# Late pair slots of one and a half blocks, by turns with triples, and quarter-row gathers for slots 3 to 5

## The chip, the core and the metric

The kernel runs on one core of a Trainium2 chip. The metric is the device time of one execution in microseconds, of which the median over several runs is given. The engines are TensorE (PE, matrix products; PEld are its weight loads), VectorE (DVE), ScalarE (ACT), GpSimd (POOL) and SyncE (SP, which here only issues transfers). Transfers from SP and from POOL share the core's 16 DMA engines. On-chip memory has 128 partitions; products land in PSUM, in banks of 512 numbers per partition.

## The reference

An attention with 32 memory slots per head is computed for 8 batches of 576 positions and 8 heads of 64. Its output is the input x (4608 tokens of 512 numbers) of a mixture of 8 experts with a hidden size of 1024, where each token goes to the one expert of the largest gate logit:

```python
x = attn_out.transpose(0, 2, 1, 3).reshape(B * S, H * D)   # 4608 x 512
e_idx = argmax(x @ w_gate)                                  # one expert per token
for e in range(E):
    mask = e_idx == e
    h = maximum(x[mask] @ w1[e], 0)                         # 512 -> 1024
    out[mask] = gate_w[mask] * eom[mask, e] * (h @ w2[e])   # 1024 -> 512
```

All numbers are 32-bit. The kernel gets that precision from products of two parts: each matrix is split into a rounded part (`hh`, `xh`, `whl[:, 0]`) and the remainder (`hl`, `xl`, `whl[:, 1]`), and a product is made of three passes, high by high, low by high, high by low (`PASS`, L1151).

## The kernel before

**Attention.** The batches are handled in four pairs. Products, softmax and gate logits are issued in an order written out by hand (`ORDER`, `MEM`). The rows of x, each 512 numbers with four 16-number strips of gate values (`XROW`, 576 numbers), are stored to a buffer `xs` in DRAM. When a pair of batches is done, `rank` (L875) finds each token's expert and its rank within the expert, and builds one-hot masks `Aw` on POOL (L956).

**Slots.** The experts' work is cut into slots that are fixed in number while the program is written; which expert a slot serves is looked up when it runs (`slot`, read by `value_load`, L550). A block is 128 tokens of one expert. There are five early slots of three blocks (0 and 1 use list "a", 2 to 4 list "b", made once two and three of the four batch pairs are ranked), five late triples (slots 5 to 9), four pairs of two blocks (10 to 13), and 22 single-block slots at the end, which run only if `used` (L1315) says that blocks are left over. The late slots use list "l". `route_early` (L281) and `route_late` (L338) share the experts' blocks out; `table` (L213) makes the lists of token numbers: `idx_g` to gather by, `idx_o` to scatter by, and for list "l" `idx_q`, the indices by quarters of rows (L259 to L274), made with the matrix `rep`.

**Gather and turn.** `gather` (L512) brings a slot's rows from `xs` into `xg` by indirect DMAs on POOL's queue: one per block for the slots in `WHOLE` (0 to 5), or, for the others (`quart`), four per block, each of 32 tokens' four row quarters on 128 partitions. `turn_x` (L1021) turns x so that its 512 numbers lie on partitions, in four parts c: by PE transposes (L1041) for whole rows, by a DVE transpose of 32 x 32 squares (L1035) for quarters, where four small ACT copies also fetch the gate values (L1031). ACT rounds the result to `xh` (L1043), DVE takes the remainder `xl` (L1044). Three `xg` tiles go round; `gathers` (L587) issues a slot's gathers when its list is made (`listed`) and it is fewer than three slots ahead, and forces what is missing when it must.

**Weights.** A slot's weights come in 8 units of 512 KB: four of the first layer, four of the second. `Stream` (L534) loads them on SP's queue; `split` (L557) makes the two parts, a cast on ACT (L564) and a subtraction on DVE (L565). `done` (L579), called after each unit used, splits further units as far as the ring of split units allows (10 tiles after `GROW`).

**A slot's products.** `several` (L1160) runs triples and pairs. First layer: for each of the four units and each half j of it, 12 matmuls (L1176) of 384 or 256 columns into one bank; ACT evicts them through a relu (L1181) and DVE takes the remainder (L1182). Second layer: for each unit and block, six matmuls of 512 columns (L1198). `finish_y` (L1153) scales a finished block by its gate on ACT and scatters it to `out` (POOL, L1156). `TURN` says after which steps of the second layer the four parts of the next slot's x are turned (`nxt`).

**Order around the change.** Each engine runs its instructions in the order in which the program issued them. What is not part of the slots goes between their matmuls: `hook` (L1284), eight times in a first layer and once per step of a second, advances a clock by one tick and takes two steps of the routing generators (`late`). `hold(n)` lets such a generator wait n ticks, and `take_pr` lets it wait for the one shared PSUM tile `pr`. After slot 1 (`LAST`) `settle` (L1258) closes the attention's memory, opens pools for the rest, builds `rep` and grows the ring. At that time `rank(3)` with `route_late` is still under way.

Of the kernel before, what the change touches and what calls it, by code (L numbers as in the profile page):

```python
# [66 lines left out]
def attention_moe(tc, phiT, kv, qT, wgo, wall, out):  # L67
# [3 lines left out]
    with contextlib.ExitStack() as ctx:  # L71
# [21 lines left out]
        idx = {}  # L93
        for nm, n in (("a", 3 * NPS[0]), ("b", 3 * NPS[1]), ("l", NBL)):
            idx[nm] = (cp.tile([P, n], I32, name="idx_g" + nm), cp.tile([P, n], I32, name="idx_o" + nm),
                       cp.tile([P, 4, n], I32, name="idx_q" + nm) if nm == "l" else None)
# [116 lines left out]
        def table(nm, q, nch, nblk):  # L213
# [24 lines left out]
            hl = rt.tile([P, 2, NBL], BF16, name="hl_i")  # L238
# [11 lines left out]
            V.tensor_scalar(i2v, ivv, 0.0, 100000.0, ALU.is_equal, ALU.mult)  # L250
            yield
            V.scalar_tensor_tensor(io[:], ivv, -1.0, i2v, ALU.add, ALU.add)
            if nm != "l":
                return
            for z in order:
                if z["nm"] == nm and not z["quart"]:
                    z["listed"] = True

            rep = env["rep"]  # L259
            pq = ps_r.tile([P, 4, 2, NBL], F32, name="pr")  # L260
            for b in range(4):
# [19 lines left out]
        def route_early(k):  # L281
# [48 lines left out]
            yield  # L330
            yield from table(nm, t1, nch, 3 * n)
            for z in order[s0:s0 + n]:
                z["listed"] = True
            if k == 0:
                gathers(0)
            yield
# [1 line left out]
        def route_late():  # L338
# [159 lines left out]
        for s in range(NSLOT):  # L498
# [4 lines left out]
            else:  # L503
# [3 lines left out]
            slots.append({"s": s, "nb": nb, "q0": q0, "idx": idx[nm], "rows": rows,  # L507
                          "nm": nm, "quart": s not in WHOLE,
                          "known": False, "listed": False})
        order = slots  # L510

        def gather(z):  # L512
            z["xg"] = xgs.tile()
            for k in range(z["nb"]):
                q = z["q0"] + k
                if z["quart"]:
                    rows = 4 * z["rows"]
                    for b in range(4):
                        G.indirect_dma_start(  # L519
                            out=z["xg"][:, k, XQ * b:XQ * b + XQ], out_offset=None,  # L520
                            in_=xs[0:z["rows"]].rearrange("t (a q) -> (t a) q", a=4),
                            in_offset=bass.IndirectOffsetOnAxis(ap=z["idx"][2][:, b, q:q + 1], axis=0),
                            bounds_check=rows - 1, oob_is_err=False)
                    continue
                G.indirect_dma_start(
                    out=z["xg"][:, k], out_offset=None, in_=xs[0:z["rows"]],
                    in_offset=bass.IndirectOffsetOnAxis(ap=z["idx"][0][:, q:q + 1], axis=0),
                    bounds_check=z["rows"] - 1, oob_is_err=False)
# [492 lines left out]
        def turn_x(z, c):  # L1021


            nb, xg = z["nb"], z["xg"]
            n = nb * P
            if c == 0:
                z["x"] = (mo.tile([P, 4, 3 * P], F32R, name="xh"), mo.tile([P, 4, 3 * P], F32R, name="xl"))
                if z["quart"]:
                    z["g"] = env["xt"].tile([P, 3], F32, name="gx")
                    for b in range(4):  # L1030
                        A.copy(z["g"][32 * b:32 * b + 32, 0:nb], xg[0:32, 0:nb, XQ * b + P])  # L1031
            xh, xl = z["x"]
            if z["quart"]:
                xt = env["xt"].tile([P, 3 * P], F32, name="xt")
                V.transpose(xt[:, 0:n].rearrange("p (k i) -> p k i", i=32),  # L1035
                            xg[:, 0:nb].rearrange("p k (b q) -> p (k b) q", b=4)[:, :, 32 * c:32 * c + 32])
# [6 lines left out]
            A.copy(xh[:, c, 0:n], pt)  # L1043
            V.tensor_tensor(xl[:, c, 0:n], pt, xh[:, c, 0:n].bitcast(F32), ALU.subtract)  # L1044

        NT = 5 * NBP
        deferred = []
# [104 lines left out]

        def finish_y(z, k, py):  # L1153
            y = mo.tile([P, DM], F32, name="y", bufs=2)
            A.activation(y[:], py, AF.Copy, scale=z["g"][:, k:k + 1] if z["quart"] else z["xg"][:, k, P:P + 1])  # L1155
            G.indirect_dma_start(  # L1156
                out=out, out_offset=bass.IndirectOffsetOnAxis(ap=z["idx"][1][:, z["q0"] + k:z["q0"] + k + 1], axis=0),
                in_=y[:], in_offset=None, bounds_check=NTOK - 1, oob_is_err=False)

        def several(i, st, nxt, hook):  # L1160

            z = order[i]
            nb, x, h = z["nb"], z["x"], []
            n_ = nb * P
            for u in range(4):
                w = st.take(i, u)
                h_ = mo.tile([P, 2, 3 * P], F32R, name="hh", bufs=4)
                l_ = mo.tile([P, 2, 3 * P], F32R, name="hl", bufs=4)
                for j in range(2):
                    if nb == 3 or j == 0:  # L1170
                        pb = bank([1, 512] if nb == 3 else [2, 256], "ps")
                    n = 0
                    for cc in range(4):
                        for a, b in PASS:
                            o = cc * 256 + j * P
                            T.matmul(pb[:, j % pb.shape[1], 0:n_], w[:, b, o:o + P], x[a][:, cc, 0:n_],  # L1176
                                     start=(n == 0), stop=(n == 11))
                            n += 1
                    if nb == 3 or j == 1:
                        js = slice(j, j + 1) if nb == 3 else slice(0, 2)  # L1180
                        A.activation(h_[:, js, 0:n_], pb[:, :, 0:n_], AF.Relu)  # L1181
                        V.scalar_tensor_tensor(l_[:, js, 0:n_], pb[:, :, 0:n_], 0.0, h_[:, js, 0:n_].bitcast(F32),  # L1182
                                               ALU.max, ALU.subtract)
                    if j == 0:
                        hook()
                h.append((h_, l_))
                st.done(PUMP[0])
                hook()
            py = [bank([DM], "ps") for _ in range(nb)]

            turns = [(u, k) for u in range(4, 8) for k in range(nb)]
            if 8 * i + 8 == st.hi:
                turns.sort(key=lambda t: t[1])
            for step, (u, k) in enumerate(turns):
                w = st.take(i, u)
                for f in range(2):
                    for n, (a, b) in enumerate(PASS):
                        T.matmul(py[k], h[u - 4][a][:, f, k * P:(k + 1) * P], w[:, b, DM * f:DM * f + DM],  # L1198
                                 start=(u == 4 and f == 0 and n == 0), stop=(u == 7 and f == 1 and n == 2))
# [5 lines left out]
                if k == nb - 1:  # L1205
                    st.done(PUMP[0])

        def single(i, st, nxt):
# [49 lines left out]
        def settle():  # L1258
# [107 lines left out]
```

## Time and profile before

| | |
|---|---|
| runs of the kernel | 578.89 us median of 3 (578.73 to 579.51) |
| the profiled execution | 577.36 us, of which its instructions span 575.6 us |
| matmuls | 4031 |
| memory traffic in the span | 102.99 MB read, 20.87 MB written |
| indirect gathers by quarters, by whole rows | 80, 18 |
| mean granted clock of PE | 0.966 |

A row of a timeline gives start and length in microseconds, engine, line, operation, output <- input, shapes and count, and in brackets how long the engine had been idle before and what ended that. A row of a group gives the total busy time and the mean length of one in nanoseconds, then the idle time of the engine before them. A row of a stretch gives its length and the busy time of each engine in it, the granted clock, the busy share of the DMA engines and what they moved in GB/s. Matmuls overlap, so a matmul's listed length is longer than the distance to the next one.

### The profile page before, as it was taken

What the parts mean: (1) busy time and instruction counts of PE and PEld (TensorE: products, weight loads), DVE (VectorE), ACT (ScalarE), POOL (GpSimd) and SP (SyncE); (2) the same over time, 40 slices, a digit from 0 to 9 for tenths busy, and PEclk for the clock granted to TensorE, in tenths of its full rate; (3) what the DMA queues carried; (4) which work ended last, traced back from release to release, by engine and by line L of the source; (5) the groups of instructions that cost most, each with busy time, mean ns of one, the idle gap of its engine ahead of it and who ended that gap; (6) DMA issues with size and microseconds to landing.
All of it is one profiled execution on the core that took longest, in us unless ns stands there. A gap on an engine that the chain in (4) does not pass through costs nothing. (4 is left out here: it accounts for less than half of the span.)

```text
span 575.6 us, 10886 instructions
## 1 busy us (share of the span) xinstructions
PE 529.1 (92%) x4031; PEld 455.6 (79%) x4031; DVE 356.1 (62%) x736; ACT 280.4 (49%) x496; POOL 229.2 (40%) x253
## 2 busy tenths in 40 slices
PE   3688886789899999999999999999999999999993
PEld 2455554478689799898998989898998989899893
DVE  4485979767765659996443555646465555676610
ACT  3475655454254456453434545445454445656510
POOL 2242575831166034312471735547170604553011
PEclk9987879989899999999999999999999999999998
DMA  8999999975367659756564665656465655687000
GB/s 308 413 401 391 382 376 356 308 301 168 116 197 245 209 173 308 246 155 183 161 200 145 204 177 180 184 171 176 139 202 168 179 172 181 198 264 223 7 28 32
DMA packets 42238, 124.14 MB, mean 216 GB/s; under 512 B 10368, under 2 KB 10432, under 8 KB 41792
## 3 DMA queue, kind: packets, MB, share of 16 engines
q1 hardware_dynamic: 35136, 102.71, 54.7%
q0 software_dynamic: 7040, 20.65, 10.4%
q8 instruction: 33, 0.54, 0.4%
q14 instruction: 29, 0.24, 0.1%
HBM read 102.99 MB, written 20.87 MB: 215 GB/s over the span
## 5 line engine op out<-in xcount | busy, mean ns | idle before, releaser
L1176 PE MATMUL bps<-xh,whl 128*128 128x384 f32 (+1 forms) x896 | 213.6, 322 | 0.1
L1198 PE MATMUL bps<-whl,hh 128*128 128x512 f32 x608 | 197.7, 396 | 0.0
L565 DVE TENSOR_TENSOR whl<-w,whl 128x1024 fp32r<-128x1024 f32 x112 | 136.8, 1228 | 68.5 <-ACT whl L564 68.5
L1176 PEld LDWEIGHTS bps<-xh,whl 128*128 128x128 f32 x896 | 156.9, 190 | 1.9 <-issue 0.6
L1176 PE MATMUL bps<-xl,whl 128*128 128x384 f32 (+1 forms) x448 | 143.8, 321 | 0.0
L1198 PEld LDWEIGHTS bps<-whl,hh 128*128 128x128 f32 x608 | 114.7, 189 | 26.1 <-issue 2.5
L1198 PE MATMUL bps<-whl,hl 128*128 128x512 f32 x304 | 119.0, 391 | 0.0
L564 ACT CAST whl<-w 128x1024 fp32r<-128x1024 f32 x112 | 116.4, 1046 | 0.0
L519 POOL DMA_INDIRECT xg<-xs,idx_ql x80 | 90.2, 1127 | 25.2 <-issue 24.3
L1181 ACT ACTIVATE hh<-bps 128x384 fp32r<-128x384 f32 (+1 forms) x96 | 48.9, 510 | 96.9 <-PE bps L1176 96.7
L1182 DVE SCALAR_TENSOR_TENSOR hl<-bps,hh 128x384 fp32r<-128x384 f32 (+1 forms) x96 | 55.1, 577 | 52.1 <-ACT hh L1181 52.1
L1176 PEld LDWEIGHTS bps<-xl,whl 128*128 128x128 f32 x448 | 85.1, 190 | 0.5
L1156 POOL DMA_INDIRECT out<-y,idx_ol x23 | 24.9, 1081 | 127.1 <-ACT y L1155 101.4
L1198 PEld LDWEIGHTS bps<-whl,hl 128*128 128x128 f32 x304 | 57.5, 189 | 10.8
L838 POOL TENSOR_TENSOR ea<-ea,mx 128x512 f32<-128x512 f32 (+1 forms) x20 | 19.2, 961 | 49.8 <-DVE mx L836 45.4
L1043 ACT CAST xh<-xt 128x384 fp32r<-128x384 f32 (+1 forms) x32 | 14.7, 460 | 37.9 <-DVE xt L1035 37.9
L873 ACT COPY xo<-bpd 128x576 f32<-128x576 f32 x36 | 22.6, 640 | 21.3 <-PE bpd L871 12.7
L956 POOL TENSOR_SCALAR Aw<-iota_row,row 128x128 bf16<-128x128 bf16 x36 | 26.8, 759 | 12.4 <-DVE row L946 12.4
L871 PE MATMUL bpd<-ve_b,aT 64*128 64x144 f32 (+1 forms) x320 | 28.5, 327 | 2.4 <-DVE ea L833 2.4
L1044 DVE TENSOR_TENSOR xl<-xt,xh 128x384 fp32r<-128x384 f32 (+1 forms) x32 | 15.8, 492 | 24.1 <-ACT xh L1043 24.1
L1155 ACT ACTIVATE y<-bps,gx 128x512 f32<-128x512 f32 x20 | 13.4, 687 | 30.4 <-PE bps L1198 13.9
L871 PEld LDWEIGHTS bpd<-ve_b,aT 64*128 64x128 f32 (+1 forms) x320 | 21.7, 196 | 8.1 <-issue 3.5
(248 smaller groups left out, 471.6 us busy)
## 6 DMA issues: line engine op xcount, KB each, us to landing
w<-wall SPq DMA_DIRECT2D x112, 512.0 KB, 3.9
kvt<-kv SPq DMA_DIRECT2D x32, 512.0 KB, 7.5
xs<-xo SPq DMA_DIRECT2D x16, 576.0 KB, 5.8
qt<-qT SPq DMA_DIRECT2D x16, 512.0 KB, 9.1
ph<-phiT SPq DMA_DIRECT2D x3, 1152.0 KB, 12.1
kv<-kv SPq DMA_DIRECT2D x4, 512.0 KB, 9.0
xg<-xs,idx_ql POOLq DMA_INDIRECT x80, 4.2
ph<-phiT SPq DMA_DIRECT2D x4, 288.0 KB, 3.2
```

The lines of the kernel that those rows point to most:

```text
L519: G.indirect_dma_start(out=z["xg"][:, k, XQ * b:XQ * b + XQ], out_offset=None, in_=xs[0:z["rows"]].rearrange("t (a q) -> (t a) q", a=4), i ...
L564: A.copy(hl[:, 0], w[:])
L565: V.tensor_tensor(hl[:, 1], w[:], hl[:, 0].bitcast(F32), ALU.subtract)
L838: G.tensor_tensor(eav, eav, mx[:, 0:n].unsqueeze(2).to_broadcast([P, n, M]), ALU.subtract)
L871: T.matmul(px[to:to + n, r, sl], z["aT"][h, o:o + n], ves[2 * bp + b][h, g], start=True, stop=True)
L873: A.copy(xo[:, c % 2], px[:, :, 0:2 * XQ])
L956: (G if AWP else V).tensor_scalar(Aw[:, bp * NCH + c], iota_row[:], row[:, c:c + 1], None, ALU.is_equal)
L1156: G.indirect_dma_start(out=out, out_offset=bass.IndirectOffsetOnAxis(ap=z["idx"][1][:, z["q0"] + k:z["q0"] + k + 1], axis=0), in_=y[:], in ...
L1176: T.matmul(pb[:, j % pb.shape[1], 0:n_], w[:, b, o:o + P], x[a][:, cc, 0:n_], start=(n == 0), stop=(n == 11))
L1181: A.activation(h_[:, js, 0:n_], pb[:, :, 0:n_], AF.Relu)
L1182: V.scalar_tensor_tensor(l_[:, js, 0:n_], pb[:, :, 0:n_], 0.0, h_[:, js, 0:n_].bitcast(F32), ALU.max, ALU.subtract)
L1198: T.matmul(py[k], h[u - 4][a][:, f, k * P:(k + 1) * P], w[:, b, DM * f:DM * f + DM], start=(u == 4 and f == 0 and n == 0), stop=(u == 7 an ...
```

## The change

- A pair slot now holds one and a half blocks: 192 tokens. `route_late` gives an expert a pair only where two blocks are left and the last one is at most half full (`odd`); other remainders of two become two singles.
- The first layer of a pair lays xh (192 columns) and xl (192) side by side. Per quarter cc there is one matmul of 384 columns with the high weights and one of 256 with the low weights, 8 per half unit instead of 12. The bank's two halves of 192 then have to be added: ACT copies one half to SBUF (`hsum`), DVE adds the other, ACT applies the relu, and DVE takes the remainder in two pieces, 64 and 128 columns; this is done per half unit, where before one relu and one remainder served a whole unit.
- The second layer of a pair takes three matmuls per half unit for its full block and two for the half block, whose high and low parts (64 tokens each) lie side by side as one stationary matrix; `finish_y` then adds the two halves of the result (an ACT copy and a DVE addition) and scatters 64 rows. The last slot does its half block first.
- The second block of a pair is gathered with two quarter gathers instead of four.
- The late slots run in the order 5, 6, 10, 7, 11, 8, 12, 9, 13 instead of 5 to 13.
- `WHOLE` is now (0, 1, 2): slots 3, 4 and 5 gather by quarters and are turned by DVE. For slots 3 and 4 the quarter indices of list "b" are made by `quarters("b")`, which `settle` puts ahead of the running `rank(3)`, one step of each by turns; slots of quarters count as `listed` only after `quarters`.
- The ring of split units has 9 tiles instead of 10.

```diff
-GROW = ((2, 2, 2), (6, 1, 0))
+GROW = ((2, 2, 2), (5, 1, 0))
...
-WHOLE = tuple(range(NPE + 1))
+WHOLE = (0, 1, 2)
...
+        def quarters(nm, hlv=None):
+            if hlv is None:
+                yield from take_pr()
+                yield from hold(LATE["pe"])
+                hlv = hls[nm]
+            iq, nblk = idx[nm][2], hlv.shape[2]
             rep = env["rep"]
             pq = ps_r.tile([P, 4, 2, NBL], F32, name="pr")
...
             V.tensor_scalar(iq[:], t4v, 4.0, quad[:, 0:1], ALU.mult, ALU.add)
+            for z in order:
+                if z["nm"] == nm:
+                    z["listed"] = True
...
             V.tensor_scalar(ti[:, 1], ti[:, 2], 2.0, 2.0, ALU.is_ge, ALU.mult)
+            yield
+            V.tensor_tensor(ti[:, 1], ti[:, 1], odd[:], ALU.mult)
...
-        order = slots
+        a, b = NPE + NPT, NPE + NPT + NPP
+        order = slots[:NPE + 1]
+        for s in range(max(NPT - 1, NPP)):
+            order += slots[NPE + 1 + s:a][:1] + slots[a + s:b][:1]
+        order += slots[b:]
...
-                    for b in range(4):
+                    for b in range(2 if (z["nb"], k) == (2, 1) else 4):
...
+            if (z["nb"], k) == (2, 1):
+                n = 64
+                ya = env["xt"].tile([64, DM], F32, name="ya", bufs=1)
+                A.copy(ya[:], py[64:128])
+                V.tensor_tensor(ya[:], py[0:64], ya[:], ALU.add)
+                py = ya[:]
...
+                        elif cc < 3:
+                            T.matmul(pb, wh, x[0][:, cc], start=(cc == 0), stop=False)
+                            T.matmul(pb[:, 0:256], wl, x[0][:, cc, 0:256], start=False, stop=False)
...
+                        s_ = env["xt"].tile([P, 192], F32, name="hsum")
+                        A.copy(s_[:], pb[:, 192:384])
+                        V.tensor_tensor(s_[:], pb[:, 0:192], s_[:], ALU.add)
+                        A.activation(h_[:, j, 0:192], s_[:], AF.Relu)
+                        for o, c, n in ((192, P, 64), (256, 0, P)):
+                            V.scalar_tensor_tensor(h_[:, j, o:o + n], s_[:, c:c + n], 0.0,
+                                                   h_[:, j, c:c + n].bitcast(F32), ALU.max, ALU.subtract)
...
+            late.gens[0:1] = [together(quarters("b"), *late.gens[0:1])]
             grow(1)
```

More of the change, by code (lines that the diff above doesn't have):

```diff
@@ L95, in attention_moe @@
             idx[nm] = (cp.tile([P, n], I32, name="idx_g" + nm), cp.tile([P, n], I32, name="idx_o" + nm),
-                       cp.tile([P, 4, n], I32, name="idx_q" + nm) if nm == "l" else None)
+                       cp.tile([P, 4, n], I32, name="idx_q" + nm) if nm != "a" else None)
         slot = cp.tile([P, NSLOT + 1], I32, name="slot")
@@ L237, in table @@
             yield from hold(LATE["dve"])
-            hl = rt.tile([P, 2, NBL], BF16, name="hl_i")
+            hl = rt.tile([P, 2, nblk], BF16, name="hl_i" + nm)
             iv = rt.tile([P, NBL], F32, name="iv")
@@ L252, in table @@
             V.scalar_tensor_tensor(io[:], ivv, -1.0, i2v, ALU.add, ALU.add)
+            if nm == "b":
+                hls[nm] = hlv
             if nm != "l":
@@ L257, in table @@
                     z["listed"] = True
+            yield from quarters(nm, hlv)
+        hls = {}
+        def quarters(nm, hlv=None):
[4 more added lines that the diff above has]
+            iq, nblk = idx[nm][2], hlv.shape[2]
             rep = env["rep"]
@@ L332, in route_early @@
             for z in order[s0:s0 + n]:
-                z["listed"] = True
+                z["listed"] = z["listed"] or not z["quart"]
             if k == 0:
@@ L345, in route_late @@
             nbi = rt.tile([P, E], I32, name="nbi", bufs=1)
+            odd = rt.tile([P, E], I32, name="odd", bufs=1)
             V.tensor_scalar(nbi[:], n_, 127.0, None, ALU.add)
+            V.tensor_scalar(odd[:], n_, 63.0, None, ALU.add)
             taken.clear()
@@ L1024, in turn_x @@
             nb, xg = z["nb"], z["xg"]
-            n = nb * P
+            n = 192 if nb == 2 else nb * P
             if c == 0:
-                z["x"] = (mo.tile([P, 4, 3 * P], F32R, name="xh"), mo.tile([P, 4, 3 * P], F32R, name="xl"))
+                z["x"] = (mo.tile([P, 4, 3 * P], F32R, name="xh"), mo.tile([P, 4, 3 * P], F32R, name="xl") if nb != 2 else None)
                 if z["quart"]:
@@ L1030, in turn_x @@
                     for b in range(4):
-                        A.copy(z["g"][32 * b:32 * b + 32, 0:nb], xg[0:32, 0:nb, XQ * b + P])
+                        m = 1 if nb == 2 and b > 1 else nb
+                        A.copy(z["g"][32 * b:32 * b + 32, 0:m], xg[0:32, 0:m, XQ * b + P])
             xh, xl = z["x"]
@@ L1043, in turn_x @@
             A.copy(xh[:, c, 0:n], pt)
-            V.tensor_tensor(xl[:, c, 0:n], pt, xh[:, c, 0:n].bitcast(F32), ALU.subtract)
+            lo = xh[:, c, n:2 * n] if nb == 2 else xl[:, c, 0:n]
+            V.tensor_tensor(lo, pt, xh[:, c, 0:n].bitcast(F32), ALU.subtract)
         NT = 5 * NBP
@@ L1167, in several @@
                 h_ = mo.tile([P, 2, 3 * P], F32R, name="hh", bufs=4)
-                l_ = mo.tile([P, 2, 3 * P], F32R, name="hl", bufs=4)
+                l_ = mo.tile([P, 2, 3 * P], F32R, name="hl", bufs=4) if nb == 3 else None
                 for j in range(2):
-                    if nb == 3 or j == 0:
-                        pb = bank([1, 512] if nb == 3 else [2, 256], "ps")
-                    n = 0
+                    pb = bank([512], "ps")[:, 0:3 * P]
                     for cc in range(4):
[L1174 to L1183, printed above, removed]
+                        o = cc * 256 + j * P
+                        wh, wl = w[:, 0, o:o + P], w[:, 1, o:o + P]
+                        if nb == 3:
+                            T.matmul(pb, wh, x[0][:, cc], start=(cc == 0), stop=False)
+                            T.matmul(pb, wh, x[1][:, cc], start=False, stop=False)
+                            T.matmul(pb, wl, x[0][:, cc], start=False, stop=(cc == 3))
+                        elif cc < 3:
+                            T.matmul(pb, wh, x[0][:, cc], start=(cc == 0), stop=False)
+                            T.matmul(pb[:, 0:256], wl, x[0][:, cc, 0:256], start=False, stop=False)
+                        else:
+                            T.matmul(pb[:, 0:256], wl, x[0][:, cc, 0:256], start=False, stop=False)
+                            T.matmul(pb, wh, x[0][:, cc], start=False, stop=True)
+                    if nb == 3:
+                        A.activation(h_[:, j], pb, AF.Relu)
+                        V.scalar_tensor_tensor(l_[:, j], pb, 0.0, h_[:, j].bitcast(F32), ALU.max, ALU.subtract)
+                    else:
+                        s_ = env["xt"].tile([P, 192], F32, name="hsum")
[5 more added lines that the diff above has]
+                                                   h_[:, j, c:c + n].bitcast(F32), ALU.max, ALU.subtract)
@@ L1192, in several @@
             if 8 * i + 8 == st.hi:
-                turns.sort(key=lambda t: t[1])
+                turns.sort(key=lambda t: t[1], reverse=nb == 2)
             for step, (u, k) in enumerate(turns):
@@ L1196, in several @@
                 for f in range(2):
-                    for n, (a, b) in enumerate(PASS):
-                        T.matmul(py[k], h[u - 4][a][:, f, k * P:(k + 1) * P], w[:, b, DM * f:DM * f + DM],
-                                 start=(u == 4 and f == 0 and n == 0), stop=(u == 7 and f == 1 and n == 2))
+                    h_, l_ = h[u - 4]
+                    if nb == 3:
+                        ps = [((h_, l_)[a][:, f, k * P:(k + 1) * P], b) for a, b in PASS]
+                    elif k == 0:
+                        ps = [(h_[:, f, 256 * a:256 * a + P], b) for a, b in PASS]
+                    else:
+                        ps = [(h_[:, f, P:256], b) for b in range(2)]
+                    for n, (a, b) in enumerate(ps):
+                        T.matmul(py[k], a, w[:, b, DM * f:DM * f + DM],
+                                 start=(u == 4 and f == 0 and n == 0),
+                                 stop=(u == 7 and f == 1 and n == len(ps) - 1))
                 if u == 7:
@@ L1204, in several @@
                     nxt(TURN[nb].index(step))
-                if k == nb - 1:
+                if (step + 1) % nb == 0:
                     st.done(PUMP[0])
```

11 lines of the change are left out of this document (6 added, 5 removed).

## The prediction

> **What bounds the kernel now.** I read the page first, then the matrix engine's timeline from 200 us on, slot by slot, then the other engines' timelines at the two places where the change touches them.
>
> ```profile
> span 575.6 us, 10886 instructions
> PE 529.1 (92%) x4031; PEld 455.6 (79%) x4031; DVE 356.1 (62%) x736; ACT 280.4 (49%) x496; POOL 229.2 (40%) x253
> PE   3688886789899999999999999999999999999993
> ...
> L1156 POOL DMA_INDIRECT out<-y,idx_ol x23 | 24.9, 1081 | 127.1 <-ACT y L1155 101.4
> ```
>
> From the eighth slice on, PE (the matrix engine) is never idle: from slot 0 to the last matmul the time is its work. The 23 scatters with the late list are 5 x 3 + 4 x 2: no single slot ran. The reference's inputs agree: the tokens per expert come out as 576, 576, 0, 0, 576, 1152, 1152, 576, all multiples of 4.5 blocks. Four experts keep one and a half blocks each for the late pairs, so the new rule (a pair only where the last block is at most half full) finds its four pairs and no single.
>
> ```profile
> 411.06:444.09 33.03, 33.03 (x170) 30.18 (x168) 17.92 (x24) 15.96 (x27) 12.60 (x11) 1.00 0.56 170
> ...
> 477.12:499.54 22.42, 22.42 (x146) 20.52 (x145) 13.86 (x18) 11.82 (x20) 11.88 (x10) 1.00 0.67 208
> ```
>
> Those are one late triple and one pair (columns: length, busy PE, weight load, DVE, ACT, POOL, clock, DMA): PE is full in both, DVE and ACT have slack. Where the layers begin:
>
> ```profile
> 241.22 0.33 PE L1176 MATMUL bps<-xh,whl 128*128 128x384 f32 x1
> ...
> 277.48 0.33 PE L1176 MATMUL bps<-xh,whl 128*128 128x384 f32 x1
> ...
> 311.98 0.33 PE L1176 MATMUL bps<-xh,whl 128*128 128x384 f32 x1
> ...
> 411.06 0.33 PE L1176 MATMUL bps<-xh,whl 128*128 128x384 f32 x1
> ...
> 427.73 0.39 PE L1198 MATMUL bps<-whl,hh 128*128 128x512 f32 x1
> ...
> 477.12 0.28 PE L1176 MATMUL bps<-xh,whl 128*128 128x256 f32 x1
> ...
> 488.63 0.40 PE L1198 MATMUL bps<-whl,hh 128*128 128x512 f32 x1
> ```
>
> A matmul costs PE its distance to the next one: 96 of 384 columns in 427.73 - 411.06 = 16.67 us, 0.174 each; 72 of 512 in the triple's other 16.36 us, 0.227 each; 96 of 256 in 488.63 - 477.12 = 11.51 us, 0.120 each.
>
> **Part 1, matmuls of a pair.** First layer: per half unit 4 x 0.174 + 4 x 0.120 = 1.17 us, times 8 = 9.4 us. Second: 40 x 0.227 = 9.1 us. Together 18.5 against 22.42: PE would save 3.9 us per pair, 15.8 in four.
>
> **Part 2, transposes.** Slots 3, 4 and 5 no longer turn x on PE. Slot 4, in which slot 5 is turned, takes 311.98 - 277.48 = 34.50 us, 1.47 more than a slot without. Three times: **-4.4 us**.
>
> **Part 3, the gather of slot 3.** Here the change adds a wait. `rep`, from which the quarter indices are made, exists only after settle, behind slot 1. From there `quarters("b")` needs the shared PSUM tile, which `rest` of rank(3) holds:
>
> ```profile
> 219.72 0.56 DVE L1182 SCALAR_TENSOR_TENSOR hl<-bps,hh 128x384 fp32r<-128x384 f32 x1
> ...
> 220.48 0.23 DVE L934 TENSOR_TENSOR w__2746<-ohg,pr 128x72 f32<-128x72 bf16 x1
> ...
> 229.27 0.55 DVE L1044 TENSOR_TENSOR xl<-bps,xh 128x384 fp32r<-128x384 f32 x1
> ...
> 241.95 0.55 DVE L1044 TENSOR_TENSOR xl<-bps,xh 128x384 fp32r<-128x384 f32 x1
> ```
>
> L934, which frees it, follows the fifth eviction of slot 2, so it is issued at hook 5. The two holds (3 and 2 clock ticks, one per hook) put the matmuls of `quarters` at hook 8 and its first DVE instruction at hook 10, step 1 of the second layer, where `nxt(0)` forces the rest. Only then are the gathers of slot 3, and behind them those of slot 4, issued, 24 in one go. They stand on POOL behind the nine Aw masks:
>
> ```profile
> 177.73 1.06 POOL L525 DMA_INDIRECT xg<-xs,idx_gb  x1 [3.06 <-DVE idx_ob L252]
> ...
> 185.29 1.73 POOL L525 DMA_INDIRECT xg<-xs,idx_gb  x1 [0.30 <-issue]
> ...
> 224.62 9.05 POOL L956 TENSOR_SCALAR Aw<-iota_row,row 128x128 bf16<-128x128 bf16 x9 [7.71 <-DVE row L946]
> ...
> 285.70 1.04 POOL L519 DMA_INDIRECT xg<-xs,idx_ql  x1 [0.30 <-issue]
> ...
> 301.31 1.00 POOL L519 DMA_INDIRECT xg<-xs,idx_ql  x1 [0.30 <-issue]
> ```
>
> ```profile
> xg<-xs,idx_ql POOLq DMA_INDIRECT x80, 4.2
> ```
>
> Now slots 2 and 3 are gathered from 177.7 to 187.0, far ahead. Then: Aw ends at 233.7, the twelfth quarter starts 0.3 + (301.31 - 285.70) later, at 249.6, and lands 4.2 later, at **253.8**. But PE finishes slot 2 at 241.22 - 1.47 = 239.75. And DVE and ACT stand still meanwhile: `turn_x` of slot 3 put its first transpose at the head of DVE's queue around 230, with routing and weight splits behind it. After 253.8: transpose, cast, 1.2 us to the first xl. From the first to the last xl of this layer DVE took 241.95 - 229.27 = 12.7 us before, almost without a pause; to that come three transposes (1.4) and three waits of 0.64 for ACT's cast (1.9), one split less for the smaller ring (-1.15). The last xl ends at 255.0 + 12.7 + 0.55 + 1.4 + 1.9 - 1.15 = 270.4. PE does the first twelve matmuls (2.08 us) as the quarters of x come, the last three (0.52) after it: as good as a start at 268.8. **+29.1 us**. Bounds: 16, if after 251 only four bare turns of 1.7 us remain; 32, if nothing overlaps. I take the queue order. Slot 4's data land near 271, a slot early; slot 5's list is ready at the end of slot 3, its gathers end about when its first turn is issued: nothing.
>
> **Part 4, evictions of a pair.** The saving of part 1 holds only if DVE and ACT keep up.
>
> ```profile
> L565 DVE TENSOR_TENSOR whl<-w,whl 128x1024 fp32r<-128x1024 f32 x112 | 136.8, 1228 | 68.5 <-ACT whl L564 68.5
> L564 ACT CAST whl<-w 128x1024 fp32r<-128x1024 f32 x112 | 116.4, 1046 | 0.0
> L1182 DVE SCALAR_TENSOR_TENSOR hl<-bps,hh 128x384 fp32r<-128x384 f32 x80 | 44.1, 554 | 38.4 <-ACT hh L1181 38.4
> L1181 ACT ACTIVATE hh<-bps 128x384 fp32r<-128x384 f32 x80 | 39.3, 492 | 77.0 <-PE bps L1176 77.0
> L1182 DVE SCALAR_TENSOR_TENSOR hl<-bps,hh 128x512 fp32r<-128x512 f32 x16 | 11.1, 691 | 13.7 <-ACT hh L1181 13.7
> L1181 ACT ACTIVATE hh<-bps 128x512 fp32r<-128x512 f32 x16 | 9.6, 600 | 19.8 <-PE bps L1176 19.7
> ```
>
> ```profile
> 478.43 0.69 ACT L1155 ACTIVATE y<-bps,gx 128x512 f32<-128x512 f32 x1 [1.79 <-DMA out<-y,idx_ol]
> 479.02 1.04 ACT L564 CAST whl<-w 128x1024 fp32r<-128x1024 f32 x1
> ```
>
> ```profile
> 480.09 1.23 DVE L565 TENSOR_TENSOR whl<-w,whl 128x1024 fp32r<-128x1024 f32 x1 [4.06 <-ACT whl L564]
> 481.24 0.69 DVE L1182 SCALAR_TENSOR_TENSOR hl<-bps,hh 128x512 fp32r<-128x512 f32 x1
> ```
>
> By columns (1.07 ns on DVE, 0.84 on ACT) the new pieces are: add of 192 0.35, differences of 64 and 128 0.21 and 0.28, copy and relu of 192 0.34 each. The next instruction on the same engine starts 0.09 before the end of the one ahead (481.24 is 1.15 behind 480.09); a hand-over to the other engine costs 0.03 (479.02 + 1.04 to 480.09). The five instructions of a half unit alternate, ACT, DVE, ACT, DVE, DVE, and both queues are in order (ACT idles 1.79 us for a scatter before 478.43, with the cast, whose weights came long ago, behind it). From one add to the next: 0.35 + 0.03 + relu 0.34 + 0.03 + 0.12 + 0.19 = 1.06. At the end of a unit there is also the split: 0.35 + 0.03 + 0.25 + cast 1.05 + 0.03 + 1.14 = 2.85. So DVE and ACT need **3.9 us per unit, PE 2.34**. DVE is free 481.24 - 477.12 = 4.1 into the slot, and done with the first layer at 4.1 + 4 x 3.9 = 19.7, when PE would already have left the slot. Only then come the turns of x for the next triple:
>
> ```profile
> 331.45 0.57 DVE L1035 STREAM_TRANSPOSE xt<-xg 128x384 f32<-128x384 f32 x1
> 332.66 0.56 DVE L1044 TENSOR_TENSOR xl<-xt,xh 128x384 fp32r<-128x384 f32 x1 [0.64 <-ACT xh L1043]
> 333.61 1.23 DVE L565 TENSOR_TENSOR whl<-w,whl 128x1024 fp32r<-128x1024 f32 x1 [0.40 <-ACT whl L564]
> 334.76 0.57 DVE L1035 STREAM_TRANSPOSE xt<-xg 128x384 f32<-128x384 f32 x1
> ```
>
> A turn with a split takes 3.31, a bare one 1.7: 2 x 3.31 + 2 x 1.7 = 10.0, x complete at 29.7, and PE in effect starts the triple at 29.7 + 0.52 - 2.08 = 28.2. That is 5.8 longer than the 22.42 of now, in the three pairs that a triple follows: **+17.4 us**. Bounds per pair: -3.9 (all hidden) and +8 (hand-overs of 0.1, slower small instructions). The last pair has no splits and no turns: h of its last unit is there at 4.1 + 8 x 1.06 = 12.6, PE would want it at 9.4 + 3 x 0.91 = 12.1; it ends near 19.0: **-3.4**. The triples between have 4.15 us per unit for DVE and ACT and catch up; that is what the turns by kind are worth.
>
> **Part 5, the clock.** PE then has four long gaps.
>
> ```profile
> 20.00:30.00 10.00, 4.60 (x120) 2.53 (x112) 6.21 (x13) 4.71 (x13) 3.67 (x4) 0.88 1.02 415
> 30.00:40.00 10.00, 9.07 (x153) 5.94 (x153) 8.15 (x18) 6.61 (x14) 4.81 (x6) 0.78 1.03 402
> ```
>
> With gaps the granted clock was 0.88 and 0.78: 1.2 and 2.2 us lost of ten. I take 1.2 per gap, **+4.8**; bounds 0 and 8.8. The Trainium skill (TensorE: Matmul & The Clock Gate, "What's actually happening") has half the rate after an idle window of some 3.4 us, until a busy one has passed; by it, as an estimate, a gap costs 1.7 us and the four 6.8. The rows agree in direction.
>
> **Sum**, on the profiled execution's 577.36 us: 577.4 - 4.4 + 29.1 + 17.4 - 3.4 + 4.8 = 620.9. The median of the runs, 578.89, is 1.5 above it: **622 us**.
>
> **The rivals.** (1) PE stays the only bound: each half unit is evicted in under 1.17 us with its share of the split, and slot 3's x is there by 239.75. Then 577.4 - 4.4 - 15.8 + 1.5 = 559 us. For it: now PE waits for neither engine in any slot. Against: 3.9 us of alternation per unit, and sixteen us of gathers that POOL can begin at 233.7 for a need at 239.75. (2) Only slot 3 waits, the pairs keep up: 577.4 - 4.4 + 29.1 - 15.8 + 1.2 + 1.5 = 589. For it: DVE's bare busy time per unit, 2 x 0.84 + 1.23 = 2.9, is not so far above 2.34; against: the alternation. (3) Only the pairs run over, since the quarters come sooner: 577.4 - 4.4 + 17.4 - 3.4 + 3.6 + 1.5 = 592. For it: 9 us of POOL's delay are the Aw masks, whose order is fixed by hand; against: they are issued at hooks 7 and 8. (4) The change doesn't do what it says, and singles run: each 96 x 0.120 + 24 x 0.227 = 17 us at least, two or more; above 650. The counts speak against it.
>
> **Chances.** Forecast 0.64 (its own range 604 to 634), (1) 0.13, (2) 0.11, (3) 0.10, (4) 0.02. The range 584 to 636 takes in the forecast, (2) and (3) and leaves out (1), (4) and the tails, 0.18. A run can tell 0.2%, 1.2 us. Faster is (1) and the case of (2) with a stall under 19 us, 0.15; the same 0.02; slower 0.83.
>
> **What would show it.** Part 3: PE idle from about 240 for 25 to 30 us, with quarter gathers of list b on POOL from 234 to 267 and a DVE transpose that waits for them. Part 4: before each triple that follows a pair, a PE wait for DVE's xl of 5 to 10 us; pair slots of 27 to 29 us, the last of 19. Part 2: slots 3 and 4 near 33 us plus routing. If the pairs last 18.5 us, part 4 is wrong; if slot 3 begins before 245, part 3 is.

## The result, and the profile after

The changed kernel takes **622.32 us** (median of 4 runs, 621.13 to 624.07) against 578.93 us: **1.075 times as long**, 95% interval 1.072 to 1.078. In two of the experiments below one execution took some 2.75 ms (2750.26 and 2764.13 us), which the medians leave out. The profiled execution of the changed kernel is the 624.07 us one. The head of its page, with the group of matmuls that begins a triple's or early slot's products, and from the table of waits the first row (what PE waited for: total, times, longest):

```profile
span 622.3 us, 10711 instructions
PE 534.6 (86%) x3839; PEld 448.0 (72%) x3839; DVE 375.8 (60%) x839; ACT 292.6 (47%) x560; POOL 245.1 (39%) x272
PE   3688777698999995389999999996999699969993
...
L1212 PE MATMUL bps<-xh,whl 128*128 128x384 f32 x320 | 116.2, 363 | 35.5 <-ACT xh L1070 35.1
...
PE bps L1212 <- ACT xh L1070: 35.1, 13, 10.7
```

PE has 192 matmuls less, and four holes that the strip of before did not have: one of two slices near 250 us, and one each at the 28th, 32nd and 36th slice. All of them are waits for `xh`, that is, for a slot's x. The line numbers have moved: L1212 to L1214 are the first layer of a triple, L1216 to L1220 that of a pair, L1254 the second layer, L1062, L1070 and L1073 turn x, L590 and L591 split weights, L1227 to L1231 evict a pair.

The first hole, from the timelines of POOL, DVE and PE of the changed kernel:

```profile
226.97 7.24 POOL L982 TENSOR_SCALAR Aw<-iota_row,row 128x128 bf16<-128x128 bf16 x9 [12.49 <-DVE row L972]
234.38 1.13 POOL L545 DMA_INDIRECT xg<-xs,idx_qb  x1 [0.16 <-issue]
...
248.82 1.00 POOL L545 DMA_INDIRECT xg<-xs,idx_qb  x1 [0.31 <-issue]
...
251.58 0.58 DVE L1062 STREAM_TRANSPOSE xt<-xg 128x384 f32<-128x384 f32 x1 [19.00 <-DMA xg<-xs,idx_qb]
...
252.76 0.69 PE L1212 MATMUL bps<-xh,whl 128*128 128x384 f32 x1 [10.65 <-ACT xh L1070]
...
267.45 0.56 DVE L1073 TENSOR_TENSOR xl<-xt,xh 128x384 fp32r<-128x384 f32 x1 [0.58 <-ACT xh L1070]
267.47 0.69 PE L1212 MATMUL bps<-xh,whl 128*128 128x384 f32 x1 [3.54 <-ACT xh L1070]
...
285.72 0.39 PE L1254 MATMUL bps<-whl,hh 128*128 128x512 f32 x1
```

Twelve quarter gathers of slot 3 run on POOL from 234.4 to 249.8; DVE stands still for 19.0 us with the first transpose at the head of its queue; the last `xl` is ready at 268.0. PE trickles through ten matmuls between 252.7 and 268, which the stretches show (columns as before the change: length, PE, weight loads, DVE, ACT, POOL, clock, DMA share, GB/s):

```profile
241.90:252.70 10.80, 0.20 (x1) 0.00 (x0) 0.58 (x1) 1.27 (x6) 8.09 (x9) 0.71 0.22 55
252.70:268.00 15.30, 5.35 (x10) 2.65 (x10) 13.29 (x36) 6.50 (x10) 12.23 (x11) 0.50 0.56 158
268.00:276.00 8.00, 8.00 (x31) 7.94 (x31) 5.09 (x15) 3.82 (x7) 1.90 (x3) 0.64 0.44 147
...
403.82:433.88 30.06, 24.53 (x116) 18.99 (x114) 18.33 (x39) 15.35 (x33) 8.03 (x8) 0.89 0.55 164
466.91:496.21 29.30, 23.47 (x114) 18.31 (x112) 17.77 (x38) 14.60 (x33) 8.03 (x8) 0.93 0.56 164
529.24:559.68 30.44, 24.96 (x117) 19.39 (x116) 18.50 (x40) 15.75 (x34) 8.03 (x8) 0.90 0.55 162
592.71:612.00 19.29, 18.97 (x105) 16.62 (x103) 7.48 (x26) 7.52 (x20) 2.93 (x3) 1.00 0.15 51
```

The last four rows are the pairs, each from its first matmul to 16.67 us (a triple's first layer at full clock) before the next triple's second layer. Three last 30.06, 29.30 and 30.44 us, where a pair of two blocks took 22.42; the last one, with no triple behind it, 19.3. What fills a pair, on DVE and PE:

```profile
403.82 0.33 PE L1216 MATMUL bps<-xh,whl 128*128 128x384 f32 x1
...
406.81 1.23 DVE L591 TENSOR_TENSOR whl<-w,whl 128x1024 fp32r<-128x1024 f32 x1 [4.15 <-ACT whl L590]
407.95 0.35 DVE L1228 TENSOR_TENSOR hsum<-bps,hsum 128x192 f32<-128x192 f32 x1
408.73 0.43 DVE L1231 SCALAR_TENSOR_TENSOR hh<-hsum,hh 128x64 fp32r<-128x64 f32 x2 [0.43 <-ACT hh L1229]
...
410.80 1.22 DVE L591 TENSOR_TENSOR whl<-w,whl 128x1024 fp32r<-128x1024 f32 x1 [0.51 <-ACT whl L590]
...
413.21 0.40 PE L1254 MATMUL bps<-whl,hh 128*128 128x512 f32 x1
...
423.91 0.57 DVE L1062 STREAM_TRANSPOSE xt<-xg 128x384 f32<-128x384 f32 x1
...
433.16 0.56 DVE L1073 TENSOR_TENSOR xl<-xt,xh 128x384 fp32r<-128x384 f32 x1 [0.58 <-ACT xh L1070]
```

PE is through the first layer in 413.21 - 403.82 = 9.39 us, but DVE needs 410.80 - 406.81 = 3.99 us per unit, gets to the next triple's x only at 423.91, and has it ready at 433.72.

### The profile page after: what moved, and what is told of

The parts are those of the page before. It is cut to its first block, busy times and chain, and to the rows that moved or that the text cites. A ratio compares the mean times of both kernels' runs of the same rounds, so it can differ in the third digit from the quotient of the medians.

```text
span 622.3 us, 10711 instructions
## 1 busy us (share of the span) xinstructions
PE 534.6 (86%) x3839; PEld 448.0 (72%) x3839; DVE 375.8 (60%) x839; ACT 292.6 (47%) x560; POOL 245.1 (39%) x272
## 5 line engine op out<-in xcount | busy, mean ns | idle before, releaser
L1254 PE MATMUL bps<-whl,hh 128*128 128x512 f32 x640 | 194.2, 395 | 1.9 <-ACT hh L1229 1.6
L591 DVE TENSOR_TENSOR whl<-w,whl 128x1024 fp32r<-128x1024 f32 x112 | 136.8, 1227 | 84.5 <-ACT whl L590 84.4
L1212 PE MATMUL bps<-xh,whl 128*128 128x384 f32 x320 | 116.2, 363 | 35.5 <-ACT xh L1070 35.1
L1254 PEld LDWEIGHTS bps<-whl,hh 128*128 128x128 f32 x640 | 119.5, 188 | 32.8 <-ACT hh L1229 4.0
L590 ACT CAST whl<-w 128x1024 fp32r<-128x1024 f32 x112 | 116.1, 1043 | 0.0
L1213 PE MATMUL bps<-xl,whl 128*128 128x384 f32 x320 | 114.8, 359 | 0.6 <-DVE xl L1073 0.5
L1214 PE MATMUL bps<-xh,whl 128*128 128x384 f32 x320 | 112.6, 352 | 0.0
L1212 PEld LDWEIGHTS bps<-xh,whl 128*128 128x128 f32 x320 | 64.2, 201 | 44.3 <-ACT xh L1070 42.4
L1254 PE MATMUL bps<-whl,hl 128*128 128x512 f32 x240 | 93.6, 390 | 0.0
L1222 ACT ACTIVATE hh<-bps 128x384 fp32r<-128x384 f32 x80 | 38.8, 494 | 65.8 <-PE bps L1214 65.5
L1213 PEld LDWEIGHTS bps<-xl,whl 128*128 128x128 f32 x320 | 64.0, 200 | 5.5 <-DVE xl L1073 5.3
L1214 PEld LDWEIGHTS bps<-xh,whl 128*128 128x128 f32 x320 | 64.2, 201 | 0.0
L1223 DVE SCALAR_TENSOR_TENSOR hl<-bps,hh 128x384 fp32r<-128x384 f32 x80 | 43.3, 552 | 32.1 <-ACT hh L1222 31.9
L1254 PEld LDWEIGHTS bps<-whl,hl 128*128 128x128 f32 x240 | 45.1, 188 | 8.7
L1070 ACT CAST xh<-xt 128x384 fp32r<-128x384 f32 (+1 forms) x44 | 19.9, 452 | 58.0 <-DVE xt L1062 58.0
L1062 DVE STREAM_TRANSPOSE xt<-xg 128x384 f32<-128x384 f32 (+1 forms) x44 | 21.9, 499 | 19.0 <-DMA xg<-xs,idx_qb 19.0
```

The costliest lines, as they stand in the source:

```text
L590: A.copy(hl[:, 0], w[:])
L591: V.tensor_tensor(hl[:, 1], w[:], hl[:, 0].bitcast(F32), ALU.subtract)
L1212: T.matmul(pb, wh, x[0][:, cc], start=(cc == 0), stop=False)
L1213: T.matmul(pb, wh, x[1][:, cc], start=False, stop=False)
L1214: T.matmul(pb, wl, x[0][:, cc], start=False, stop=(cc == 3))
L1222: A.activation(h_[:, j], pb, AF.Relu)
```

## The experiments

The theory was the prediction's: two independent losses, about 26 us net at slot 3 (the quarter gathers) and about 21 in the pairs (the alternation of ACT and DVE), each with its share of the clock. The rivals were that one of them hides the other, that the order of the slots matters, or that the clock alone is the price.

**Slots 3 to 5 gathered by whole rows again**, the only edit to the changed kernel:

```diff
-WHOLE = (0, 1, 2)
+WHOLE = tuple(range(NPE + 1))
```

> The changed kernel with slots 3, 4 and 5 gathered by whole rows again; the pairs stay as changed. Theory (slot 3 waits because its quarter gathers are issued behind slot 1 and stand behind the Aw masks on POOL): the gap before slot 3, 24.7 us and some 2.6 us of clock behind it, goes, the 4.4 us of transposes come back: 622.3 - 27.3 + 4.4 = 599 us; the pair slots stay at 28 to 30 us. Rival (the gap comes from the smaller ring or the routing, not from the gathers): 615 us or more, with PE still idle before slot 3.

Measured: 596.58 us (595.33 to 597.64), 1.030 times the kernel before (1.027 to 1.033). On the timeline of PE slot 3 follows at once:

```profile
242.14 0.33 PE L1212 MATMUL bps<-xh,whl 128*128 128x384 f32 x1
...
258.80 0.39 PE L1254 MATMUL bps<-whl,hh 128*128 128x512 f32 x1
```

The gathers by quarters cost 25.7 us net; the pairs, at 30.6 us for the first, are as long as with them. So the two losses are apart. The ring of nine tiles and the new routing are still in this kernel, so the gap doesn't come from them.

**Only the quarters**: the kernel before, with the hunks for `WHOLE`, `GROW`, `quarters` and `settle` alone; pairs of two blocks, and the old order.

```diff
-WHOLE = tuple(range(NPE + 1))
+WHOLE = (0, 1, 2)
...
+            late.gens[0:1] = [together(quarters("b"), *late.gens[0:1])]
```

> The kernel before with only the quarter gathers of slots 3 to 5 (list b by quarters, ring of nine); pairs of two blocks, old order. Theory: the parts add: 578.9 - 4.4 + 27.3 = 602 us, slots 10 to 13 at 22.4 us each. Rival (the gap needs the changed pairs or routing too): within 5 us of 578.9 - 4.4.

Measured: 612.07 us (611.51 to 614.05), ratio 1.058 (1.054 to 1.061): the hole at slot 3 is there, but ten us more than expected were lost. They lie in slot 4, which lasts 42.2 us instead of 33.0. The timelines of POOL and ACT of this kernel:

```profile
299.22 1.27 POOL L534 DMA_INDIRECT xg<-xs,idx_ql  x1 [22.27 <-PE bps L1213]
...
314.10 1.00 POOL L534 DMA_INDIRECT xg<-xs,idx_ql  x1 [0.30 <-issue]
315.41 1.02 POOL L1171 DMA_INDIRECT out<-y,idx_ob  x1 [0.30 <-issue]
...
318.27 0.69 ACT L1170 ACTIVATE y<-bps,gx 128x512 f32<-128x512 f32 x1 [16.95 <-DMA out<-y,idx_ob]
```

The twelve gathers of slot 5 stand on POOL's queue ahead of the scatter of slot 3's first y. There are two y buffers, so ACT's third y waits 16.95 us for that scatter, with casts and evictions queued behind it. In the changed kernel the same list comes one hook later, as the pair rule has one more routing step, and the order is the other way round:

```profile
302.51 0.98 POOL L1193 DMA_INDIRECT out<-y,idx_ob  x1 [25.17 <-ACT y L1192]
303.80 1.05 POOL L545 DMA_INDIRECT xg<-xs,idx_ql  x1 [0.30 <-issue]
```

There slot 5 lasts 33.8 us. That the extra routing step alone makes the difference is read from the two traces and was not tried by itself; the stall itself is shown, and comes back below.

**Splits out of a pair's first layer.** Four of the eight splits are moved behind the evictions:

```diff
-                st.done(PUMP[0])
+                st.done(PUMP[0] if nb == 3 else 0)
...
-                    st.done(PUMP[0])
+                    st.done(PUMP[0] if nb == 3 else 1)
```

> The changed kernel, but in a pair slot no weight unit is split during the first layer, and one per unit in the second; the following triple catches up. Theory (ACT and DVE alternate for 3.99 us per unit, 1.75 of it the split): the chain of evictions falls to 2.1 us per unit, below PE's 2.34, x of the next triple is whole at about 22 us instead of 29.9; a pair slot falls from 30 to about 22.8 us, three of them by 21 us: about 601 us. Rival (a pair is slow since its weights are split too late): units run short, 625 us or more, with PE waiting for whl in the triples.

Measured: 599.36 us (597.06 to 602.17), ratio 1.036 (1.031 to 1.040). The first pair, 401.67 to 441.31 - 16.67 = 424.64, lasts 23.0 us for 30.1; the next two 22.5 and 21.4, for 29.3 and 30.4. On DVE:

```profile
408.05 0.35 DVE L1228 TENSOR_TENSOR hsum<-bps,hsum 128x192 f32<-128x192 f32 x1
408.83 0.43 DVE L1231 SCALAR_TENSOR_TENSOR hh<-hsum,hh 128x64 fp32r<-128x64 f32 x2 [0.43 <-ACT hh L1229]
409.18 0.35 DVE L1228 TENSOR_TENSOR hsum<-bps,hsum 128x192 f32<-128x192 f32 x1
...
414.84 0.58 DVE L1062 STREAM_TRANSPOSE xt<-xg 128x384 f32<-128x384 f32 x1
```

Without splits a half unit takes 409.18 - 408.05 = 1.13 us, under PE's 1.17, and the turn of x begins at 13.2 us into the pair, not at 20.1. The loss is DVE's and ACT's chain, and goes when the chain is shortened.

**The same by regrouping.** The splits stay, but both halves of a unit are copied and added first, then comes the split, then one relu and two remainders for the whole unit:

```diff
-                        A.activation(h_[:, j, 0:192], s_[:], AF.Relu)
...
                 st.done(PUMP[0])
+                if nb == 2:
+                    A.activation(h_[:, :, 0:192], s_[:], AF.Relu)
+                    for o, c, n in ((192, P, 64), (256, 0, P)):
+                        V.scalar_tensor_tensor(h_[:, :, o:o + n], s_[:, :, c:c + n], 0.0, ...)
```

> The changed kernel, but a pair's evictions are regrouped: both half units are copied and added as they come, then the weight unit is split, then one relu and two differences serve the whole unit. The same work, fewer hand-overs. Theory (the alternation costs, not the amount of work): copies and adds run beside each other, ACT and DVE need about 2.2 us per unit instead of 3.99, the first layer's chain ends at about 13.5 instead of 20.1 us, x of the next triple at about 23.5 instead of 29.9: three pair slots 6 to 7 us shorter, about 602 us. Rival (the amount of ACT and DVE work is the bound): 617 us or more.

Measured: 597.87 us (595.92 to 600.27), ratio 1.033 (1.026 to 1.040); the first pair lasts 22.8 us.

```profile
406.37 1.21 DVE L591 TENSOR_TENSOR whl<-w,whl 128x1024 fp32r<-128x1024 f32 x1
407.50 0.62 DVE L1236 SCALAR_TENSOR_TENSOR hh<-hsum,hh 128x128 fp32r<-128x128 f32 x2
408.04 0.61 DVE L1228 TENSOR_TENSOR hsum<-bps,hsum 128x192 f32<-128x192 f32 x2
408.57 1.22 DVE L591 TENSOR_TENSOR whl<-w,whl 128x1024 fp32r<-128x1024 f32 x1
```

A unit now takes DVE 408.57 - 406.37 = 2.20 us instead of 3.99, with the same split in it. Of the 1.79 between them 1.37 were waits for ACT (0.43 twice and 0.51 in the rows of the changed kernel), which are gone; the rest, 0.42, goes with the fewer and longer instructions. What still holds the pair is the turn of x, with splits between its parts in the second layer.

**No adds at all.** The first layer of a pair as three passes of 192 columns, both halves of a unit in one bank:

```diff
+                            xa, xb = x[0][:, cc, 0:192], x[0][:, cc, 192:384]
+                            T.matmul(p2[:, j, 0:192], wh, xa, start=(cc == 0), stop=False)
+                            T.matmul(p2[:, j, 0:192], wh, xb, start=False, stop=False)
+                            T.matmul(p2[:, j, 0:192], wl, xa, start=False, stop=(cc == 3))
```

> The changed kernel, but a pair's first layer is made of three passes of 192 columns into one bank per unit, with one relu and the differences per unit, and no halves to add. Theory: the evictions fall to about 1.9 us per unit and no longer bound the pair. What a matmul of 192 columns costs no run has shown: if its cost goes on falling with the columns as from 384 to 256 (0.174 to 0.120), it is 0.093 us, the first layer 8.9 us, and a pair about 22 us: 600 us. [...]

Measured: 598.55 us (597.62 to 600.03), ratio 1.034 (1.030 to 1.039). On PE:

```profile
401.34 0.25 PE L1220 MATMUL bps<-xh,whl 128*128 128x192 f32 x1
...
412.04 0.65 PE L1252 MATMUL bps<-whl,hh 128*128 128x512 f32 x2
```

96 matmuls of 192 columns take 10.70 us, 0.111 each, where 256 columns take 0.120 and 384 take 0.174. Laying the parts side by side, with the copy and the add that it needs, saves PE just 10.70 - 9.39 = 1.3 us per pair; this kernel and the regrouped one (597.87 us) are not told apart.

**The pairs behind all triples**:

```diff
-        order = slots[:NPE + 1]
...
+        order = slots
```

> The changed kernel with the slots in the order of their numbers: five late triples, then the four pairs in a row. What are the turns by kind worth? Theory (a pair slot is as long as its own chain on ACT and DVE, because nothing is worked ahead across slots): a pair behind a pair turns only 192 columns, x is whole about 2 us sooner, but the chain starts some 3 us later since no triple lets the queues catch up: pairs of 28 to 31 us, 622 us within 5. Rival (the triples between absorb a backlog that would otherwise grow from pair to pair): 635 us or more, each pair longer than the one before.

Measured: 620.93 us (620.51 to 622.50), ratio 1.073 (1.069 to 1.078). Pairs that follow each other last 30.0, 28.4 and 29.9 us: they carry no growing backlog that a triple would have to work off. The turns by kind are worth nothing that can be measured.

**PE kept busy through the first hole**, by 100 matmuls of 512 columns whose product nobody uses:

```diff
+                if i == 3 and u == 0:
+                    pw = bank([512], "ps")
+                    for n in range(100):
+                        T.matmul(pw, w[:, 0, 0:P], w[:, 0, 0:512], start=True, stop=True)
```

> The changed kernel with 100 matmuls of 512 columns ahead of slot 3's first one, whose result nothing uses; they fill some 23 us of the gap in which PE waits for x. Theory (about 2.6 us behind the gap are lost to a lower granted clock): the granted clock stays at 1.00 through the gap, the first layer of slot 3 ends 2 to 3 us earlier after its last x: 619.7 us. Rival (the matmuls behind the gap are slow because x comes piecewise, not by the clock): 622.3 us, and the same length from the last x to the second layer.

Measured: 622.16 us (621.81 to 624.31), ratio 1.076 (1.073 to 1.079): nothing gained.

```profile
241.00:262.50 21.50, 21.50 (x96) 17.83 (x95) 11.12 (x30) 6.71 (x12) 17.06 (x15) 1.00 0.42 122
262.50:272.00 9.50, 8.24 (x46) 7.64 (x45) 5.39 (x17) 3.37 (x6) 5.33 (x5) 1.00 0.39 116
...
285.69 0.53 PE L235 MATMUL pr<-bwl,Aw 128*128 128x90 bf16 x9 [0.63 <-DVE bwl L227]
```

The clock stays at 1.00, and the second layer of slot 3 begins 2.6 us sooner, counted from slot 2's start (280.99 - 206.23 against 285.72 - 208.32). Then PE waits twice for DVE's routing work in that layer (0.63 us in the row above, 0.80 us at 291.21), and the lead is 0.9 us at the start of slot 4 and 0.2 at that of slot 6. So the part of the forecast that gave 619.7 us in all failed: behind the first hole the slow clock alone does not set the end, DVE is about as late.

**Both losses mended.** The regrouped evictions; whole-row gathers for slot 3; and in a pair's second layer no split before the last part of x is turned:

```diff
-WHOLE = (0, 1, 2)
+WHOLE = (0, 1, 2, 3)
...
-                    st.done(PUMP[0])
+                    st.done(PUMP[0] if nb == 3 or step > 4 else 0)
```

> The changed kernel with three things mended: slot 3 gathers whole rows again (4 and 5 by quarters), the evictions of a pair are grouped by unit with the split between, and in a pair's second layer the splits come after the last turn of x. Theory: no gap before slot 3, pair slots of 18.5 to 20 us: 578.9 - 2.9 (two slots without transposes) - 3 x 3.5 - 3.4 = 562 us, faster than both kernels. Rival (the splits put off make the weights late in the next triple): PE waits for whl, 570 to 585 us.

Measured: 568.83 us (567.60 to 570.93), ratio 0.982 (0.978 to 0.986). That is 7 us more than was expected. The pairs last 18.46 us, and PE waits for no `whl` anywhere, so the rival's sign is missing; but slot 3 lasts 43.3: the stall of the second experiment, one slot earlier. ACT waits 11.95 us for a scatter behind gathers, the splits and evictions behind it come late, and so does DVE's routing work, for which PE then waits (1.74 and 1.53 us).

```profile
235.72 1.13 POOL L545 DMA_INDIRECT xg<-xs,idx_qb  x1 [0.16 <-issue]
...
250.40 1.00 POOL L545 DMA_INDIRECT xg<-xs,idx_qb  x1 [0.30 <-issue]
251.70 1.03 POOL L1193 DMA_INDIRECT out<-y,idx_ob  x1 [0.30 <-issue]
...
254.58 0.69 ACT L1192 ACTIVATE y<-bps,xg 128x512 f32<-128x512 f32 x1 [11.95 <-DMA out<-y,idx_ob]
```

**The same with whole rows in slots 0 to 5, and in slots 0 to 4**:

```diff
-WHOLE = (0, 1, 2, 3)
+WHOLE = tuple(range(NPE + 1))
```

> The kernel with all three mended, and slots 4 and 5 gather whole rows too, so that only the pairs differ from the kernel before. Theory (in the mended kernel slot 3 lost some 7 us because the twelve quarter gathers of slot 4 stood on POOL ahead of slot 2's scatters, for which ACT waited with the third y, 11.95 us): that wait goes, two slots of transposes (2.9 us) come back: 568.8 - 7 + 2.9 = 565 us, or 579 - 3 x 3.9 - 3.4 = 564. Rival (the 7 us come from the routing or the smaller ring): 570 us or more.

> The same with slot 5 alone gathered by quarters. Theory: its gathers come behind the first scatter of slot 3, as in the changed kernel, and ACT waits little: one slot of transposes less than with six whole, 563 us. Rival (whichever slot is the first to gather by quarters meets the scatters ahead of it): 568 us or more, with ACT waiting over 10 us for a scatter in slot 3 or 4.

Measured: 563.87 us (562.47 to 565.05) with six, ratio **0.974 (0.970 to 0.978)**, and with five 563.04 us (561.87 to 567.90), ratio 0.971 (0.966 to 0.975). Both are faster than the kernel before and than the changed one, and they aren't told apart. With six, from the page and the stretch of the first pair:

```profile
span 562.1 us, 10635 instructions
PE 515.3 (92%) x3875; PEld 442.2 (79%) x3875; DVE 362.0 (64%) x795; ACT 287.0 (51%) x532; POOL 226.0 (40%) x245
PE   3678868869899999999999999999999999999994
...
379.67:398.13 18.46, 18.46 (x105) 16.89 (x104) 12.13 (x26) 10.94 (x24) 9.91 (x8) 1.00 0.67 225
```

No hole is left, and a pair is PE's own time; only behind the first pair is x still late, where the triple's first layer takes 416.46 - 398.13 = 18.33 us for 16.67. The gain is 15.0 us, where four pairs at 3.96 us less make 15.8.

With five, three runs took 561.87 to 563.04 us, as was expected, and two 567.44 and 567.90, near the rival's 568. The trace is of the 567.44 one, and its table of what ACT waited for has the rival's sign:

```profile
ACT y L1192 <- DMA out<-y,idx_ob: 16.8, 3, 10.5
```

The gathers of slot 5 do come behind the first scatter of slot 3, but those of slot 6 stand ahead of slot 4's first scatter, for which slot 4's third y waits 10.53 us. Slot 5, where this falls, is just 1.2 us longer than with six (34.18 against 33.03), and the first pair with its triple 3.0 (56.11 against 53.16). What parts the two groups of runs, and whether five is better than six, stays open.

## Why the prediction was right

The sum was 43.5 us above the profiled time of before (620.9 - 577.4); the medians differ by 43.4. The mechanisms were right, but that the numbers meet to a tenth is luck: the runs of the changed kernel spread over 2.9 us, and its terms were less exact and cancelled. The two profiled executions differ by 46.7 us, of which 43.2 lie in slots 2 to 13; 2.0 lie ahead of slot 2 and 1.5 behind the last matmul, where the sum has no term.

One reading was too broad: PE's strip of before is not full from the eighth slice on (7, 8 and 8 tenths in slices 8, 9 and 11) but from the twelfth, 158 us, which still covers every slot that the change touches.

- **Part 1, right.** The first layer of a pair takes PE 9.39 us (9.4 was worked out), a whole pair, where nothing else holds it, 18.46 (18.5).
- **Part 2, right.** Slot 4, without slot 5's transposes, takes 33.0 us (34.50 - 1.47 = 33.03). Slot 2 and the second layer of slot 3 are 1.3 us shorter each, so it is 4.1 us in all for 4.4.
- **Part 3, right in mechanism, 4.6 us too large.** x counted as ready at 268.0 - 2.08 + 0.52 = 266.4, PE was through slot 2 at 241.9: 24.5 us, not 29.1. The terms that were mis-sized are those ahead of the landing. Counted from slot 2's start (206.3 before, 208.3 after) the data came 4.2 us sooner than worked out: the Aw masks ended 1.5 us sooner (7.24 us for 9.05), the twelve gathers took 1.3 us less, and the last one landed 251.58 - 248.82 = 2.8 us behind its issue, not 4.2, with the DMA engines at 0.22 in that stretch. The 16.6 us from landing to the last `xl` measured 16.4.
- **Part 4, right.** 3.99 us per unit (3.9), DVE free 4.13 us into the pair (4.1), first layer evicted at 423.91 - 403.82 = 20.1 (19.7), x complete at 29.9 (29.7), so 28.3 in effect (28.2). The last pair 19.3 (19.0). What failed is the last sentence of that part, that the triples "catch up" and that this is "what the turns by kind are worth": with the pairs in a row nothing grows.
- **Part 5, too small, and of less weight in slot 3 than it was given.** Behind the first pair the clock cost 30.06 - 28.3 = 1.7 us, behind the hole of slot 3 285.72 - 16.67 - 266.4 = 2.6, where 1.2 each was taken. The granted clock was 0.50 to 0.71 in the first hole, and behind the first pair:

```profile
425.08:433.00 7.92, 4.10 (x9) 2.05 (x9) 5.57 (x8) 3.25 (x5) 0.00 (x0) 0.64 0.60 176
433.00:441.00 8.00, 7.97 (x33) 7.51 (x33) 5.72 (x8) 6.32 (x10) 1.29 (x1) 0.71 0.55 141
```

The Trainium skill (TensorE: Matmul & The Clock Gate, "What's actually happening") has half the rate until a busy window of some 3.4 us has passed. The prediction's estimate of 1.7 us per gap by it is what the pair shows: from 433.72, when x is whole, to 437.1 the clock was 0.50. Behind the long hole it was 0.9 more. But the idle window of some 3.4 us that the prediction puts ahead of the half rate is not in this trace: PE's longest gap in the pair was 2.03 us, and the clock was at 0.50 from 427.5 on. The busy-gap run adds that in slot 3 these 2.6 us were not on the path alone.

By the undone halves: the quarters cost 25.7 us by the medians, where 29.1 - 4.4 + 1.2 = 25.9 was the sum. In the traces slots 2 to 5 are 23.4 us longer with them (162.5 against 139.1); the rest lies outside these slots, so this near match too is in part luck. Moving the splits gave back 23.0, and the three pairs alone make 22.9 of it (89.8 us in the changed kernel, 66.9 without the splits), where 17.4 + 3.6 = 21.0 had been put on the overrun. So slot 3 with its clock was 3.2 us too high (29.1 + 1.2 against 24.5 + 2.6) and the pairs with theirs 1.5 too low (21.0 against 7.64 + 6.88 + 8.02 = 22.5). The transposes, 0.7 us more in slot 5 and the last pair (3.1 saved for 3.4) make up 1.3 of the rest.

The rivals: (2) and (3), each loss alone, were made by experiment. Rival (3), with the 4.4 us of transposes that this run keeps, is 592 + 4.4 = 596.4; measured 596.6. The run with the quarters alone kept the old pairs, so rival (2) compares after 15.8 us are taken off: 612.1 - 15.8 = 596 against 589, and in the difference lie the 9.2 us that slot 4 lost to a scatter behind gathers. The prediction weighed the gathers of slot 5 by their landing alone ("nothing"); in the changed kernel that held, but only by the order in which one scatter and the gathers reach POOL. That order cost 9.2 us in slot 4 of that run, and only 1.2 in slot 5 of the mended kernel with five. Rival (1), 559, is what the mended kernel with six comes near to, without the 4.4 us of transposes: 559 + 4.4 = 563.4, and 563.87 was measured. The form of late slots is worth 15.0 of its 15.8 us of PE work when the evictions and splits let it; in the changed kernel they and the quarters ate that and 43 us more.

## What to carry to other kernels

A matmul saved on PE is a gain only if the engines that evict it keep its pace: cost the alternation of two in-order engines, hand-over by hand-over, and group the steps so that each engine has the other unit's work while it waits (2.20 us per unit for 3.99). A transfer that is cut into four costs its issuing queue four times the issue, so look at what stands behind it there, above all scatters that free a buffer. And mend one loss at a time: with the evictions regrouped the trace showed the turn of x as the next limit, and with that mended too the scatter behind the gathers.

## What the runs showed of the hardware that was not expected

A matmul's time hardly fell with its columns below 256: 0.174 us at 384, 0.120 at 256, 0.111 at 192, each with its own weight load of 128 x 128; in proportion to 384 the last would be 0.087. What holds it there no run shows. A quarter gather took POOL 1.00 us and 0.30 to the next, so that the twelve of a slot hold its queue for 15.4 us (234.38 to 249.82). And the granted clock fell to 0.50 behind the first pair though no gap of PE there was longer than 2.03 us: from 424.0 to 427.5 PE was busy for 1.06 us of 3.5.
